# Attention: the values' products of two steps in one place, and the order of the work around them

## The chip, the core and the metric

The kernel runs on one core of a Trainium2 chip, with TensorE (matrix products), VectorE, ScalarE and GpSimd as computing engines and SyncE as the queue that issues most DMAs. Each engine runs its instructions in the order in which they were written and waits on semaphores for the others. The metric is the device time of one execution in microseconds (us); lower is better. A run is the median of several executions; one further execution is recorded by the profiler.

## The reference

Three stages follow one another. Clustered attention: each query and key is assigned to the nearest of 16 centroids of its head, and only pairs with the same centroid see each other. Then a dense layer (weights given in float64), then a layer of eight experts with a gate.

```python
q_assign = np.argmax(np.einsum('bhsd,hcd->bhsc', q_n, c_n), axis=-1)
k_assign = np.argmax(np.einsum('bhsd,hcd->bhsc', k_n, c_n), axis=-1)
mask = q_assign[:, :, :, None] == k_assign[:, :, None, :]
scores = scale * np.matmul(q, k.transpose(0, 1, 3, 2))
scores = np.where(mask, scores, -1000000000.0)
scores = scores - np.max(scores, axis=-1, keepdims=True)
attn = np.exp(scores)
attn = attn / (np.sum(attn, axis=-1, keepdims=True) + 1e-09)
return np.matmul(attn, v).astype(np.float32)
...
h = x @ w_in
sp = np.where(h > 20.0, h, np.log1p(np.exp(np.minimum(h, 20.0))))
g = h * np.tanh(sp)
return (g @ w_out).astype(np.float32)
```

There are 2 batches of 8 heads, 768 positions, 64 numbers per head. The expert layer is not touched by the change.

## The kernel before

Attention works on pairs of heads, eight pairs (`i` from 0 to 7), and each pair is cut into twelve steps: two halves of the queries (`r`, 384 each) times six blocks of 128 keys (`t`). So there are 96 steps, `s = 12*i + 6*r + t`. A step s does:

- `score(s)`: four products (lines 395 and 398, tile `pst`) into one of two large PSUM buffers that are handed out in turn, then one exponential on ScalarE (line 402) into a tile `P` in SBUF, of which there are four.
- `max_unit(n)`: one maximum of 128 queries over all keys, for a step eleven steps later: two products (line 365, tile `pm`) into the other of the two large buffers, and a reduction on VectorE (line 369). It is written first in its step.
- `pv(s-1)`: the values' product of the step before (line 428, tile `acc`). Each head's 64 columns fill half of the array, so this product runs in another arrangement of TensorE than the 128-column products around it. Behind the sixth block ScalarE copies `acc` to `x` (line 434).
- `add_up(s-1)`: two additions of `P` to the running sum on GpSimd (line 416), for the last three groups of six steps on VectorE.

Once per six steps the sums are multiplied by ones (`norm1`, line 441, tile `psum`, also 64 columns), with a logarithm and an exponential on ScalarE (lines 446, 447) to get a reciprocal `rc`; `norm2` refines it and multiplies (`rs` on VectorE, line 456, and ScalarE, line 464; `x` on GpSimd, lines 455 and 465); `norm3` splits the result in two parts (`xh` on ScalarE, line 476, `xl` on VectorE, line 477).

Once per pair the next pair but one is prepared: `load` of q and k, four `split`s (three transposes, tile `pt`, line 233; a copy on ScalarE, line 239; a subtraction on VectorE, line 240), four `sims` (products with the centroids, tile `psim`, line 251; a copy `cl` on ScalarE, line 257; an addition on VectorE, line 258), two `pick`s (a maximum and the one-hot comparison `e`, lines 267 and 268), `onehot_t` (transposes `pe`, line 277; copy `et`, line 282), two `first`s (a product `pp`, line 291, and `nf` on VectorE, line 292), and `spread`s, which are DMAs (line 353): `qa`, `ka` copy parts of q and k, `qm`, `km` copy the masks from `nf` into the tiles QA and KA that the maxima's products read. `max_put` transposes the maxima (`pmt`, line 374).

Between these, attention converts the float64 weights of the dense layer (class `Narrow`): `last` (line 718) and `bias` (line 712) on ScalarE, then `up` and `sign` on VectorE (lines 725 and 734), chunk by chunk. The small PSUM tiles (`pt`, `psim`, `pe`, `pp`, `pmt`, `psum`, and the conversion's `n32p`) share three banks in turn, so each waits until the one three places before it has been read.

What runs in which step is written out in `plan`: `at(s, f, ...)` puts the call f into step s. `advance` goes through the steps and orders the calls of one step. A function that returns a second part (the subtraction of `split`, the addition of `sims`, `nf`, `xl`) has it called at the start of the next step, behind the first maximum.

Of the kernel before, what the change touches and what calls it, by code (L numbers as in the profile page):

```python
# [169 lines left out]
class Attention:  # L170
# [310 lines left out]
    def plan(self, N):  # L481
# [5 lines left out]
        def at(s, f, *a):  # L487
            if s >= 0:
                steps.setdefault(s, []).append((f, a))
# [4 lines left out]
        for s in range(NS):  # L494
            at(s, self.score, s)
        for s in range(NS):
            at(s + 1, self.pv, s)
            at(s + 1, self.add_up, s)
            if s % 6 == 5:
                for j, f in ((3, self.norm1), (4, self.norm2), (6, self.norm3)):  # L500
                    at(s + j, f, *divmod(s // 6, 2))
        for i in range(NP):
            end = 12 * i - self.AHEAD
# [1 line left out]
                if i + r:  # L505
                    at(unit[12 * i + 6 * r + 5] + 1, self.max_put, i, r)
            base = end - 15 if i > 2 else self.B2
            if i == 1:
                at(0, self.onehot_t, i)
                for g in range(2):  # L510
                    at(1, self.first, i, g)
                for h in range(2):
                    for kind in ("km", "qm"):
                        at(2, self.spread, i, (kind, h))
            if i > 1:
                at(base - 8, self.load, i, "qk")
                for j in range(4):
                    at(base + j, self.split, i, "qk"[j // 2], j % 2)
# [26 lines left out]
        return steps  # L545

    BS = 2
    SOON, SLOTS = (14, 19, 22), (0, 2, 7, 8, 10)
    B2 = 0

    BEFORE = 8
# [85 lines left out]
    def advance(self, upto, more={}):  # L637

        for s in range(self.at, upto):
            todo = self.steps.get(s, [])  # L640
            units = [a for f, a in todo if f == self.max_unit]
            first = [a for f, a in todo if f == self.max_put and a == (0, 1)]
            for a in units[:1]:
                self.max_unit(*a)
            for a in first:
                self.max_put(*a)
            for g in self.late:
                g()
            for g in more.get(s, []):
                g()  # L650
            now = (self.score, self.norm1, self.pv, self.add_up, self.onehot_t, self.first)
            todo = [x for f in now for x in todo if x[0] == f] + [x for x in todo if x[0] not in now]
            late = [f(*a) for f, a in todo if f != self.max_unit and not (f == self.max_put and a in first)]
            for a in units[1:]:
                self.max_unit(*a)
            self.late = [g for g in late if callable(g)]
        self.at = upto


# [1075 lines left out]
```

## Time and profile before

| | |
|---|---|
| median of 3 runs | 788.06 us (787.91 to 789.1) |
| profiled execution | 787.98 us, span 786.1 us |
| TensorE products busy | 753.6 us, 96% |
| VectorE busy | 588.8 us, 75% |
| ScalarE busy | 466.6 us, 59% |
| GpSimd busy | 220.7 us, 28% |
| chain that ended last | TensorE 70%, VectorE 16%, issue 5%, ScalarE 4%, DMA 3% |

The span is the time from the first to the last instruction in the trace; the execution's own time is 1.9 us longer. A busy time is a sum over the whole program, with stages of different kinds in it: attention takes about the first third. A matrix product's time in the trace includes its way through the array, so the time between the starts of two products says more than the duration of one. In the time lines each row gives start and duration in us, the engine, the line, the operation, the tile written and the tiles read, and in brackets how long the engine was idle before it and whose end released it.

### The profile page before, as it was taken

How to read it: one execution, taken by the hardware profiler on the slowest of the kernel's cores; microseconds unless marked ns; L12 is line 12 of the kernel's file. 1: busy time of each engine (PE TensorE's matmuls, PEld its weight loads, DVE VectorE, ACT ScalarE, POOL GpSimd, SP SyncE). 2: the span in 40 equal slices, each digit the busy share in tenths (PEclk: the TensorE clock that was granted, in tenths of full speed). 3: DMA queues.
4: the chain of work that ended last, by engine and by line, in shares of the span. 5: the costliest groups of instructions: out<-in, count | busy, mean ns of one | idle time of the engine just before them, and what ended most of it. 6: DMA issues, size and time to landing. Idle time of an engine off the chain costs nothing.

```text
span 786.1 us, 12515 instructions
## 1 busy us (share of the span) xinstructions
PE 753.6 (96%) x4295; PEld 607.5 (77%) x4297; DVE 588.8 (75%) x1195; ACT 466.6 (59%) x901; POOL 220.7 (28%) x247
## 2 busy tenths in 40 slices
PE   8989999999999989899999999999999999999994
PEld 5656566666654568788989899999888999999993
DVE  6756778879779799999997688788677665666661
ACT  4445778778776766555556454445645655656651
POOL 6256668787792200010000030000231101101110
PEclk9999999999999999999999999999999999999998
DMA  9696698989793539796465456232429867986640
GB/s 200 146 218 132 164 273 249 230 237 250 202 281 120 214 128 341 256 317 229 178 233 182 140 188 196 108 141 74 135 82 282 267 213 215 276 262 222 199 125 22
DMA packets 118694, 155.78 MB, mean 198 GB/s; under 512 B 35006, under 2 KB 82206, under 8 KB 114528
## 3 DMA queue, kind: packets, MB, share of 16 engines
q1 hardware_dynamic: 113952, 131.82, 57.6%
q0 software_dynamic: 4624, 23.09, 7.4%
q8 instruction: 36, 0.59, 0.3%
q14 instruction: 34, 0.28, 0.1%
q10 hardware_dynamic: 48, 0.01, 0.0%
HBM read 93.65 MB, written 42.24 MB: 173 GB/s over the span
## 4 chain that ended last, share of the span: by engine, by line
PE 70%; DVE 16%; issue 5%; ACT 4%; DMA 3%; POOL 1%; SPq 1%; ACTq 0%; POOLq 0%; DVEq 0%
PE ph L852 12%; PE o L913 11%; PE he L1509 9%; PE y L1542 9%; PE acc L428 6%; PE pm L365 4%; PE pst L395 3%; PE pst L398 3%; PE psim L251 3%; DVE m L369 2%; DVE n L867 2%; DVE cut L810 1%; DMA n<-in_moe_w_in_dram 1%; ACT r L877 1%; PE o L1161 1%
## 5 line engine op out<-in xcount | busy, mean ns | idle before, releaser
L810 DVE TENSOR_TENSOR cut<-raw,cut 128x512 fp32r<-128x512 f32 x168 | 110.1, 686 | 26.6 <-ACT cut L809 17.6
L369 DVE TENSOR_REDUCE m<-pm 128x1 f32<-128x768 f32 x96 | 91.0, 954 | 49.3 <-PE pm L365 48.9
L416 POOL TENSOR_TENSOR sum<-sum,P 128x384 f32<-128x384 f32 x104 | 104.3, 1034 | 13.1 <-ACT P L402 10.9
L402 ACT ACTIVATE P<-pst 128x768 f32<-128x768 f32 x96 | 77.7, 809 | 43.2 <-PE pst L398 40.4
L809 ACT ACTIVATE cut<-raw 128x512 fp32r<-128x512 f32 x168 | 98.1, 623 | 2.0 <-DMA raw<-in_moe_w_dram 2.0
L1542 PE MATMUL y<-cut,hy 128*128 128x512 f32 x384 | 99.3, 394 | 0.0
L1509 PE MATMUL he<-xeh,cut 128*128 128x256 f32 x512 | 92.5, 280 | 0.2 <-ACT xeh L1463 0.2
L877 ACT ACTIVATE r<-n,two 128x384 f32<-128x384 f32 x64 | 39.5, 617 | 81.1 <-DVE n L867 80.1
L1509 PEld LDWEIGHTS he<-xeh,cut 128*128 128x128 f32 x512 | 82.2, 188 | 5.5 <-ACT xeh L1463 0.4
L428 PE MATMUL acc<-P,vn 128*64 128x384 f32 x384 | 82.4, 508 | 0.1
L1542 PEld LDWEIGHTS y<-cut,hy 128*128 128x128 f32 x384 | 67.6, 188 | 10.9
L852 PE MATMUL ph<-xh,cut 128*128 128x384 f32 x256 | 67.1, 343 | 5.8 <-DVE t L889 3.5
L1509 PE MATMUL he<-xel,cut 128*128 128x256 f32 x256 | 71.5, 279 | 0.2 <-DVE xel L1464 0.2
L395 PE MATMUL pst<-QB,KB 128*128 128x384 f32 x192 | 67.1, 349 | 4.7 <-DVE m L369 3.5
L1514 ACT ACTIVATE hy<-he 128x256 fp32r<-128x256 f32 x64 | 24.5, 383 | 71.7 <-PE he L1509 71.7
L1554 POOL DMA_INDIRECT out_dram<-ye,meta x17 | 18.3, 1077 | 171.6 <-ACT ye L1552 156.9
L852 PE MATMUL ph<-xh,again 128*128 128x384 f32 x256 | 66.1, 339 | 0.0
L398 PE MATMUL pst<-QA,KA 97*128 97x384 f32 x192 | 64.9, 338 | 0.0
L913 PE MATMUL o<-cut,gh 128*128 128x512 f32 x192 | 59.8, 392 | 1.0 <-DVE rs L456 1.0
L1515 DVE SCALAR_TENSOR_TENSOR hy<-he,hy 128x256 fp32r<-128x256 f32 x64 | 27.1, 423 | 44.7 <-ACT hy L1514 44.7
L913 PE MATMUL o<-again,gh 128*128 128x512 f32 x192 | 59.6, 392 | 0.0
L365 PE MATMUL pm<-KA,QA 96*128 96x384 f32 x192 | 54.1, 369 | 2.8 <-DVE m L369 2.7
(238 smaller groups left out, 1616.1 us busy)
## 6 DMA issues: line engine op xcount, KB each, us to landing
raw<-in_moe_w_dram SPq DMA_DIRECT2D x72, 256.0 KB
raw<-in_moe_w_dram SPq DMA_DIRECT2D x36, 512.0 KB
kept<-cut POOLq DMA_DIRECT2D x16, 1024.0 KB, 8.5
again<-kept SPq DMA_DIRECT2D x16, 1024.0 KB
n<-in_moe_w_in_dram SPq DMA_DIRECT2D x16, 512.0 KB
n<-in_moe_w_out_dram SPq DMA_DIRECT2D x16, 512.0 KB
wf<-n SPq DMA_DIRECT2D x32, 256.0 KB
raw<-wf SPq DMA_DIRECT2D x16, 512.0 KB
```

The source lines that it names most:

```text
L365: nc.tensor.matmul(ps[:, g, 0:384], lhsT=QA[0:96, h, q0:q0 + 128], rhs=KA[0:96, h, 384 * g:384 * g + 384], start=True, stop=True,)
L369: nc.vector.reduce_max(out=self.mx[r][:, 3 * h + t:3 * h + t + 1], in_=ps[:, :, 0:384], axis=AX.XY)
L395: nc.tensor.matmul(ps[:, h, 0:384], lhsT=KB[:, h, ks], rhs=QB[:, h, qs], start=True, stop=False)
L398: nc.tensor.matmul(ps[:, h, 0:384], lhsT=KA[0:97, h, ks], rhs=QA[0:97, h, qs], start=False, stop=True)
L416: e.tensor_add(out=o[:, h], in0=a[:, h], in1=b[:, h])
L428: nc.tensor.matmul(acc[64 * h:64 * h + 64, 0:384], lhsT=st["v"][:, h, t, :], rhs=pt[:, h, :], start=(t == 0), stop=(t == self.NK - 1),)
L809: nc.scalar.activation(out=t[:, 0, part], in_=raw[:, part], func=AF.Copy)
L810: self.low.tensor_sub(out=t[:, 1, part], in0=raw[:, part], in1=f32(t[:, 0, part]))
L852: nc.tensor.matmul(ps[:, 0:384], lhsT=w[:, k, :], rhs=x[:, k, sl], start=(k == 0 and j == 0), stop=(k == 3 and j == 2),)
L913: nc.tensor.matmul(self.acc[t], lhsT=g[:, c], rhs=w, start=(f == 0 and j == 0), stop=(f == self.NF - 1 and j == 2),)
L1509: nc.tensor.matmul(ps[:, 0:MAIN], lhsT=w[:, k, :], rhs=x[:, k, :], start=(k == 0 and j == 0), stop=(k == 3 and j == 2),)
L1542: nc.tensor.matmul(st["y"][s], lhsT=g[:, c], rhs=w, start=(f == 0 and j == 0), stop=(f == 7 and j == 2))
```

## The change

The constant `TWO = 24, 72` marks the steps that it rewrites.

- In them the values' product of an even step is put one step later, so that the even steps hold two (of the step two before and of the step before) and the odd steps none.
- `norm2` moves into the step of `norm1`, as the last thing in it; `norm3` comes one step earlier.
- For the pairs from 4 on the preparation is laid out anew: q and k are loaded one step earlier; the four splits stand in steps -3, -1, 1 and 2 (from `base`, instead of 0 to 3), the four centroid products in 3, 4, 5 and 7 (instead of 4 to 7), the one-hot transposes one step later, both `first`s together two and one steps later, and the masks' DMAs (`km`, `qm`) one step later.
- In even steps the second part of `split` and `sims` is called at once instead of in the next step.
- The float64 conversions go from the places 0, 2, 7, 8, 10 of each twelve steps to 1, 3, 5, 7, 10.

```diff
--- before.py
+++ after.py
@@ -494,10 +494,12 @@
         for s in range(NS):
             at(s, self.score, s)
         for s in range(NS):
-            at(s + 1, self.pv, s)
+            two = self.TWO[0] <= s < self.TWO[1]
+            at(s + 2 if two and s % 2 == 0 else s + 1, self.pv, s)
             at(s + 1, self.add_up, s)
             if s % 6 == 5:
-                for j, f in ((3, self.norm1), (4, self.norm2), (6, self.norm3)):
+                two = self.TWO[0] <= s < self.TWO[1] - 6
+                for j, f in ((3, self.norm1), (3 if two else 4, self.norm2), (5 if two else 6, self.norm3)):
                     at(s + j, f, *divmod(s // 6, 2))
         for i in range(NP):
             end = 12 * i - self.AHEAD
@@ -505,14 +507,29 @@
                 if i + r:
                     at(unit[12 * i + 6 * r + 5] + 1, self.max_put, i, r)
             base = end - 15 if i > 2 else self.B2
-            if i == 1:
+            if 12 * i > self.TWO[0] + 12:
+                at(base - 9, self.load, i, "qk")
+                for f, js in ((self.split, (-3, -1, 1, 2)), (self.sims, (3, 4, 5, 7))):
+                    for n, j in enumerate(js):
+                        at(base + j, f, i, "qk"[n // 2], n % 2)
+                at(base + 6, self.pick, i, "q")
+                at(base + 8, self.pick, i, "k")
+                at(base + 10, self.onehot_t, i)
+                for g in range(2):
+                    at(base + 12, self.first, i, g)
+                for h in range(2):
+                    for kind in ("qa", "ka"):
+                        at(base + 8, self.spread, i, (kind, h))
+                    for kind in ("km", "qm"):
+                        at(base + 13, self.spread, i, (kind, h))
+            elif i == 1:
                 at(0, self.onehot_t, i)
                 for g in range(2):
                     at(1, self.first, i, g)
                 for h in range(2):
                     for kind in ("km", "qm"):
                         at(2, self.spread, i, (kind, h))
-            if i > 1:
+            elif i > 1:
                 at(base - 8, self.load, i, "qk")
                 for j in range(4):
                     at(base + j, self.split, i, "qk"[j // 2], j % 2)
@@ -545,7 +562,8 @@
         return steps
 
     BS = 2
-    SOON, SLOTS = (14, 19, 22), (0, 2, 7, 8, 10)
+    SOON, SLOTS = (14, 19, 22), (1, 3, 5, 7, 10)
+    TWO = 24, 72
     B2 = 0
 
     BEFORE = 8
@@ -649,11 +667,24 @@
             for g in more.get(s, []):
                 g()
             now = (self.score, self.norm1, self.pv, self.add_up, self.onehot_t, self.first)
-            todo = [x for f in now for x in todo if x[0] == f] + [x for x in todo if x[0] not in now]
-            late = [f(*a) for f, a in todo if f != self.max_unit and not (f == self.max_put and a in first)]
+            two = s % 2 == 0 and self.TWO[0] <= s < self.TWO[1]
+            end = (self.norm2,) if two else ()
+            todo = (
+                [x for f in now for x in todo if x[0] == f] + [x for x in todo if x[0] not in now + end]
+                + [x for x in todo if x[0] in end]
+            )
+            self.late = []
+            for f, a in todo:
+                if f == self.max_unit or f == self.max_put and a in first:
+                    continue
+                g = f(*a)
+                if callable(g):
+                    if two and f in (self.split, self.sims):
+                        g()
+                    else:
+                        self.late.append(g)
             for a in units[1:]:
                 self.max_unit(*a)
-            self.late = [g for g in late if callable(g)]
         self.at = upto
```

How this moves instructions shows in three places; the changed file is longer, so lines 712 to 734 of the kernel before are 743 to 765 in it. On TensorE in steps 42 and 43, before (`acc` is a values' product, two for one step; `pm` maxima, `pst` scores, `pe` one-hot transposes):

```order
L428 MATMUL acc<-P,vn_1207 64x384 x2
L365 MATMUL pm<-KA_99,QA_98 128x384 x2
L395 MATMUL pst<-QB_102,KB_103 128x384
L398 MATMUL pst<-QA_96,KA_97 128x384
L395 MATMUL pst<-QB_102,KB_103 128x384
L398 MATMUL pst<-QA_96,KA_97 128x384
L428 MATMUL acc<-P,vn_1207 64x384 x2
L277 LDWEIGHTS e_1739
```

and after (`pmt` the maxima's transpose, `pt` a split's transposes):

```order
L428 MATMUL acc<-P,vn_1213 64x384 x4
L365 MATMUL pm<-KA_99,QA_98 128x384 x2
L395 MATMUL pst<-QB_102,KB_103 128x384
L398 MATMUL pst<-QA_96,KA_97 128x384
L395 MATMUL pst<-QB_102,KB_103 128x384
L398 MATMUL pst<-QA_96,KA_97 128x384
L374 MATMUL pmt<-ident,m_106 128x128
L233 MATMUL pt<-ident,qn_1633 128x128 x3
L365 MATMUL pm<-KA_99,QA_98 128x384 x2
L395 MATMUL pst<-QB_102,KB_103 128x384
```

Four products to `acc` now stand together in step 42, and step 43 has none between its scores and the next maxima.

On ScalarE around the sums of steps 43 to 45, before (`et` is the one-hot copy, `n_...` and `n32p` the conversion, `rc` the sums' logarithm and exponential, `rs` the normalisation's second part, `P` a step's exponential):

```order
L402 ACTIVATE P<-pst 128x768
L282 ACTIVATE et_105<-pe 64x768
L376 ACTIVATE mt<-pmt 6x128
L712 ACTIVATE n32p<-n_11_1602 128x512
L402 ACTIVATE P<-pst 128x768
L446 ACTIVATE rc<-psum,eps 128x384
L447 ACTIVATE rc<-rc 128x384
L718 ACTIVATE n_12_1678<-n_12_1678 128x512
L402 ACTIVATE P<-pst 128x768
L464 ACTIVATE rs<-rs,neg 128x384
```

and after:

```order
L402 ACTIVATE P<-pst 128x768
L446 ACTIVATE rc<-psum,eps 128x384
L447 ACTIVATE rc<-rc 128x384
L282 ACTIVATE et_105<-pe 64x768
L749 ACTIVATE n_12_1717<-n_12_1717 128x512
L464 ACTIVATE rs<-rs,neg 128x384
L402 ACTIVATE P<-pst 128x768
```

The one-hot copy, a conversion and the normalisation's second part now stand in one row between two exponentials.

On VectorE around the masks `nf` of pair 5, before (`m` is the reduction of the maxima, `ql` a split's subtraction, `xl` the normalisation's split):

```order
L292 TENSOR_SCALAR nf<-pp,fb 64x384
L456 SCALAR_TENSOR_TENSOR rs<-psum,rc 128x384
L369 TENSOR_REDUCE m_107<-pm 128x1
L292 TENSOR_SCALAR nf<-pp,fb 64x384
L725 SCALAR_TENSOR_TENSOR n32p<-n32p,n_12_1678 128x512
L734 SCALAR_TENSOR_TENSOR n_12_1922<-n_12_1678,n32p 128x512
L369 TENSOR_REDUCE m_107<-pm 128x1
```

and after:

```order
L240 TENSOR_TENSOR ql_1827<-pt,qh_1826 128x384
L756 SCALAR_TENSOR_TENSOR n32p<-n32p,n_12_1717 128x512
L765 SCALAR_TENSOR_TENSOR n_12_1924<-n_12_1717,n32p 128x512
L369 TENSOR_REDUCE m_107<-pm 128x1
L292 TENSOR_SCALAR nf<-pp,fb 64x384 x2
L477 SCALAR_TENSOR_TENSOR xl_75<-x,xh_73 128x384
L369 TENSOR_REDUCE m_107<-pm 128x1
```

Both halves of `nf` now stand behind the reduction that follows the conversion, and the reductions between the halves are gone.

## Rows read from the trace of the kernel before

**Rows 1.** Busy time by stretch: length, each engine (instructions), granted clock, DMA share, GB/s
```profile
97.38:222.15 124.77, 123.60 (x692) 78.97 (x692) 102.21 (x159) 96.78 (x172) 94.69 (x96) 1.00 0.90 241
222.20:250.80 28.60, 26.69 (x132) 15.10 (x131) 24.35 (x34) 19.73 (x33) 17.86 (x18) 1.00 0.60 180
```

**Rows 2.** Time line of TensorE: first score product of steps 36 and 48
```profile
128.09 0.34 PE L395 MATMUL pst<-QB,KB 128*128 128x384 f32 x1
...
159.57 0.34 PE L395 MATMUL pst<-QB,KB 128*128 128x384 f32 x1
```

**Rows 3.** Time line of TensorE (start, duration, line, tile): steps 57 to 59, 64
```profile
182.07 0.87 PE L441 MATMUL psum<-sum,ones 128*64 128x384 f32 x4
182.76 0.81 PE L428 MATMUL acc<-P,vn 128*64 128x384 f32 x4
...
187.14 0.87 PE L428 MATMUL acc<-P,vn 128*64 128x384 f32 x4
187.94 0.55 PE L233 MATMUL pt<-ident,qn 128*128 128x128 f32 x3
188.24 0.60 PE L365 MATMUL pm<-KA,QA 96*128 96x384 f32 x2
188.68 0.34 PE L395 MATMUL pst<-QB,KB 128*128 128x384 f32 x1
...
189.47 0.87 PE L428 MATMUL acc<-P,vn 128*64 128x384 f32 x4
...
201.49 0.39 PE L251 MATMUL psim<-cc,qh 128*128 128x256 f32 x1
...
202.31 0.51 PE L365 MATMUL pm<-KA,QA 96*128 96x384 f32 x2
202.66 0.34 PE L395 MATMUL pst<-QB,KB 128*128 128x384 f32 x1
```

**Rows 4.** Time lines of TensorE, ScalarE, VectorE: who waits for whose end
```profile
164.59 0.62 PE L365 MATMUL pm<-KA,QA 96*128 96x384 f32 x2 [0.32 <-DVE m L369]
...
246.53 0.79 ACT L402 ACTIVATE P<-pst 128x768 f32<-128x768 f32 x1
...
247.38 0.45 PE L395 MATMUL pst<-QB,KB 128*128 128x384 f32 x1 [0.41 <-ACT P L402]
...
248.39 0.81 ACT L402 ACTIVATE P<-pst 128x768 f32<-128x768 f32 x1 [1.06 <-PE pst L398]
...
249.28 0.96 DVE L369 TENSOR_REDUCE m<-pm 128x1 f32<-128x768 f32 x1
...
250.29 0.62 PE L365 MATMUL pm<-KA,QA 96*128 96x384 f32 x2 [1.14 <-DVE m L369]
```

**Rows 5.** Groups of instructions, 97.4 to 222.2 (total, mean ns | idle before)
```profile
L725 DVE SCALAR_TENSOR_TENSOR n32p<-n32p,n 128x512 int32<-128x512 int32 x20 | 13.8, 690 | 0.0
...
L718 ACT ACTIVATE n<-n 128x512 int32<-128x512 uint8 x20 | 13.3, 667 | 0.0
...
L464 ACT ACTIVATE rs<-rs,neg 128x384 f32<-128x384 f32 x8 | 4.9, 617 | 1.7 <-DVE rs L456 1.6
...
L282 ACT ACTIVATE et<-pe 64x768 bf16<-64x768 bf16 x4 | 3.2, 804 | 0.3
```

**Rows 6.** Time line of VectorE: one-hot comparison in steps 52 and 54
```profile
172.96 1.23 DVE L268 TENSOR_TENSOR e<-qs,mx 128x192 bf16<-128x192 f32 x1
...
178.98 0.36 DVE L268 TENSOR_TENSOR e<-ks,mx 128x192 bf16<-128x192 f32 x1
```

**Rows 7.** Time lines of the DMA queue, VectorE, TensorE: issues and first uses
```profile
0.81 0.39 SPq L128 DMA_DIRECT2D cn<-in_centroids_dram  x1
...
2.58 0.22 DVE L135 TENSOR_TENSOR cn<-cn 128x64 f32<-128x64 f32 x1 [0.72 <-DMA cn<-in_centroids_dram]
...
220.11 0.59 SPq L353 DMA_DIRECT2D QA<-nf  x1
...
223.74 0.62 PE L365 MATMUL pm<-KA,QA 96*128 96x384 f32 x2
```

## The prediction

> **What bounds the kernel now.** I read the busy time by stretch first, then TensorE's line of time step by step, then the vector and scalar engines beside it. I call the start of a step's first score product the step's start. Steps 24 to 72, which the change rewrites, run from 97.38 to 222.15: 124.8 us, 31.2 per twelve steps; TensorE is busy for 123.6 of it, VectorE for 102.2, ScalarE for 96.8 and GpSimd for 94.7, at a granted clock of 1.00, its upper level of 2.4 GHz [rows 1]. So attention is bound by TensorE, but three engines that work in strict order stand beside it at more than three quarters. The twelve steps from step 36 take 31.48 [rows 2].
>
> A bare step is three pieces [rows 3]: from the maxima's first product to the scores' first 0.44 us (0.35 where no values' product came just before), the four score products and the crossing to the values' product 0.79, and the values' product up to the next 128-column product 0.80. That is 2.03. The last two numbers hold the price of entering and leaving the 64-column arrangement. A second product inside one such episode costs less: from the sums' product to the values' product behind it is 0.69. A split's transposes cost 0.30, a centroid product 0.82 behind an episode and some 0.7 elsewhere [rows 3].
>
> **The saving on TensorE.** Two bare steps cost 4.06. With both values' products in the even step, the odd one shrinks to 0.35 + 0.70 = 1.05 (two products take 0.35, and the crossing falls away), and the even one grows to 2.03 + 0.69 = 2.72: 3.77, so 0.29 saved per pair, and 24 pairs would give 7.0 us if TensorE bounded each step. In the odd ones it doesn't.
>
> **The floor of an odd step.** Maxima and scores take turns in two PSUM buffers, so a step's scores can't start before the exponential of the step before has read its buffer. The exponential starts 1.01 after the start of scores that had to wait (their first product then lasts 0.45 instead of 0.34, so 0.90 otherwise), lasts 0.8, and the next scores start 0.06 after its end [rows 3, 4]. That makes 1.77 from scores to scores, however little TensorE has to do. Odd steps that hold a centroid product (1.05 + 0.7) fill this just so; those with a split (1.35) leave TensorE waiting 0.4, and a product that waits costs another 0.1 by the same row. The maxima have a floor of the same kind, 0.6 for the products, 0.96 for the reduction and 0.05 to the next maxima [rows 3, 4].
>
> **Twelve steps laid out.** I lay these durations on the new order, with step 36 at 0, and follow for each pair of steps what ends last.
> - 36 and 37: the even step is 3.0 (2.72 and a split). VectorE now subtracts the second split in the same step and waits for its transposes and copy until 3.4; so the reduction of step 37 starts at 3.9 instead of 3.2, and the maxima of step 38 at 4.9 instead of 4.5. Pair 5.3.
> - 38 and 39: sums' product, two values' products, centroid product, 4.2. Behind the sums ScalarE holds in a row the logarithm, the exponential, a copy that waits for the centroid product, a float64 conversion, and the normalisation's second part (0.62 [rows 5]), which waits for VectorE, which waits for that same centroid product. Only then comes step 39's exponential, 0.5 late. Pair 6.5.
> - 40 and 41: 4.6. 42 and 43: 4.6. The float64 work behind the odd maxima pushes the even reduction late, and the long even step absorbs it.
> - 44 and 45: sums, two values' products and the one-hot transposes end 3.5 after the start; then on ScalarE the one-hot copy 0.80, a conversion 0.67, the normalisation's 0.62 [rows 5], and behind them step 45's exponential, 0.6 late. Pair 6.2.
> - 46 and 47: 4.9.
> Sum 32.1, against 31.48: **plus 0.6 per twelve steps**. Against the 1.7 that six pairs save stand 1.2 from the odd floor under the three split steps, 0.5 and 0.6 from the two late exponentials, 0.4 from the late reduction and five waits of 0.1; a wait that the present order has once in twelve steps (0.32 and its 0.1 [rows 4]) is in the 31.48.
>
> **Beside GpSimd.** The one-hot comparison took 1.23 us beside GpSimd's sums and 0.36 apart from them [rows 6]. In the new order it falls into step 40, and the split of the normalised values, which I take to be of the same two kinds, into step 41, just where GpSimd, after waiting for the normalisation, catches up with its sums. Both long would push the reduction of step 42 by 0.9, of which 0.75 reaches TensorE; both short, nothing. I take 0.4, the middle. The Trainium skill's page SBUF — State Buffer (the practical consequences of its shared port pair) says that a VectorE instruction with two SBUF inputs and a GpSimd instruction that reads SBUF exclude each other for a whole instruction; by it all would be long and the time 1.4 us above my sum, while the pair of rows shows both kinds.
>
> So steps 24 to 72 change by 4 x (0.6 + 0.4) = **plus 4.0**, between plus 2.4 and plus 5.4. The first twelve still have the old normalisation, but no present wait to lose; the last twelve have no splits, but the same floor. I count them alike.
>
> **The masks' copies.** The step nf (both halves) moves behind the reduction of the step two ahead of a pair's first maxima, and the DMAs that spread it one step later, behind a float64 load. Now the copy's issue ends at 220.70, and the maxima that need it start at 223.74 without waiting for it [rows 7], so landing takes at most 3.0. The least is the centroids' load, the one small transfer whose landing a wait shows: its issue ended at 1.20, the waiting VectorE started at 2.58, 1.4 [rows 7]. In the new order the issue ends 1.7 after the start of step 48 and the maxima of step 49 want the copy at 2.6. A landing in 1.4 costs nearly nothing, since the reduction of that step is late anyway; each 0.1 more costs 0.1, at steps 37, 49, 61 and 73. Between 0.1 and 6.5 in all; I take a landing of 1.8, nearer the measured transfer: **plus 1.7**.
>
> **Behind step 72** sums run on VectorE: it is busy for 24.35 of 28.60 us, TensorE for 26.69 [rows 1], and a reduction holds the maxima for 1.14 [rows 4]. The new slots take one pair of float64 operations (2 x 0.69 [rows 5]) from step 80 to 77. Between nothing and 1.4 comes back; I take half, **minus 0.7**.
>
> **Edits at nothing.** Loads of q and k go one step earlier and stand six steps ahead of their first use instead of eight, still some 15 us. The even splits' earlier subtraction frees banks for the next sums. Products delayed by one step hold one more P buffer, three of four. Each cover is gone only if steps shrink to a third.
>
> **The sum.** The profiled run took 787.98 (the span's 786.1 and 1.9 around it), 0.08 under the median. 787.98 + 4.0 + 1.7 - 0.7 = 793.0.
>
> **Rivals.**
> (a) Faster: the odd steps keep near their floor. If the exponentials of steps 39 and 45 come on time (ScalarE's copies done some tenths sooner than my durations allow), the 1.1 goes and with it 0.5 of waits that follow: 30.5 instead of 32.1. That is 0.7 less than the present 31.2 per twelve steps, minus 2.8; with the landing hidden and minus 0.7 behind step 72, 784.5. It decides at 0.3 per odd step above the floor: below that the change gains. With every odd step at 1.77 and 19.4 for the six even ones, 30.0: minus 4.8, 782.5.
> (b) No change: half of that lateness, 786.5 to 789.5.
> (c) Much slower: the copies land at their upper end, 793.0 + 4.8 = 797.8, with all comparisons long 799.2. For it: the DMA engines are 0.90 busy there [rows 1].
> (d) The change doesn't do what it says: the second values' product pays for an episode of its own. Then 0.29 x 24 more, 800. Against it stands the 0.69.
> The Trainium skill (DMA: Bandwidth & Descriptors, on the anatomy of one DMA) gives about 2 us of fixed cost for a DMA of GpSimd's queue; as an estimate for this queue it would put the copies' term at plus 2.5 and the time at 793.8. No run here shows it for this queue.
>
> **Chances.** My forecast, slower by 2 to 8 us, 0.47; (c) 0.11; (d) 0.01; (b) 0.17; (a) 0.24. A measurement of this kernel tells some 0.2%, 1.6 us, from no change. Faster 0.24, same 0.17, slower 0.59. The range goes from 784 to 798.5.
>
> **What would show it.** Right: in the profile after, steps 24 to 72 last about 129 us; score products wait for the exponential behind odd steps, which none does there now; the exponentials of steps 39, 45, 51 and 57 start 1.4 or more after their scores; odd steps with splits last 1.8 to 1.9. Wrong: odd steps of 1.8 throughout and a stretch under 123 us mean (a); maxima that wait over 0.5 us at steps 37, 49 and 61 for copies of nf mean (c); values' products 0.8 apart inside an even step mean (d).

## The result and the profile after

| | before | after |
|---|---|---|
| median of 4 runs | 787.98 us (787.67 to 789.1) | 798.25 us (797.34 to 801.96) |
| ratio to the kernel before | | 1.0136, 95% interval 1.011 to 1.0162 |
| profiled execution, span | 787.98 us, 786.1 | 798.96 us, 797.1 |

The change makes the kernel slower by 10.3 us. The forecast was plus 5.0 with a range up to 798.5: the sign and the range held, but what came is twice what was summed. A few executions, two of the twelve with four pairs and one in each longer row of the kernel before, ran in a slower state; ratios and intervals leave them out.

The busy time by stretch (length, then the busy time and instructions of TensorE, its weight loads, VectorE, ScalarE and GpSimd, granted clock, DMA share, GB/s), for steps 24 to 72 and 72 to 84:

```profile
98.12:231.55 133.43, 124.09 (x684) 82.27 (x683) 101.66 (x158) 92.65 (x170) 95.00 (x95) 0.99 0.86 228
231.55:261.35 29.80, 27.27 (x136) 15.52 (x135) 24.30 (x35) 20.57 (x34) 18.12 (x18) 1.00 0.56 159
```

Against [rows 1] the first stretch is 8.7 us longer, yet TensorE is busy for only half a microsecond more (part of that from a few microseconds at the lower clock, below): the time went into TensorE's waits. What it waited for from 97 us to step 73 (engine and line that waited, for whose end: us in total, times, longest):

```profile
PE pm L365 <- DVE m L369: 4.1, 7, 1.2
PE pm L365 <- DMA QA<-nf: 1.9, 3, 0.9
PE pst L395 <- ACT P L402: 1.7, 4, 0.4
PE psim L251 <- DVE rs L456: 1.0, 1, 1.0
PE pm L365 <- DMA KA<-nf: 0.8, 1, 0.8
```

The same view of the kernel before has one line, the first, with 1.2 us. Three of the four others are waits that the prediction looked for, the fourth (1.0 for `rs`) is step 27, which keeps the old normalisation.

TensorE's first score products of steps 36 and 48 (start and duration in us) are 33.15 apart, where [rows 2] have 31.48:

```profile
130.21 0.44 PE L395 MATMUL pst<-QB,KB 128*128 128x384 f32 x1
...
163.36 0.44 PE L395 MATMUL pst<-QB,KB 128*128 128x384 f32 x1
```

The floor of an odd step, step 45, on TensorE's time line and on ScalarE's; a bracket is the idle time ahead and what ended it:

```profile
156.20 0.34 PE L395 MATMUL pst<-QB,KB 128*128 128x384 f32 x1
...
157.41 0.62 PE L365 MATMUL pm<-KA,QA 96*128 96x384 f32 x2
158.46 0.44 PE L395 MATMUL pst<-QB,KB 128*128 128x384 f32 x1 [0.43 <-ACT P L402]
```

```profile
157.12 0.60 ACT L464 ACTIVATE rs<-rs,neg 128x384 f32<-128x384 f32 x1
157.62 0.79 ACT L402 ACTIVATE P<-pst 128x768 f32<-128x768 f32 x1
```

The scores begin at 156.20, the exponential that empties their buffer only at 157.62, behind the one-hot copy, the conversion and the normalisation; the next scores begin at 158.46. This is the late exponential that the prediction laid out.

What it sized too small: the reduction of step 43, on VectorE's time line and, last line, TensorE's.

```profile
146.10 0.93 DVE L477 SCALAR_TENSOR_TENSOR xl<-x,xh 128x384 fp32r<-128x384 f32 x1
...
149.82 1.20 DVE L268 TENSOR_TENSOR e<-ks,mx 128x192 bf16<-128x192 f32 x1
150.94 0.94 DVE L369 TENSOR_REDUCE m<-pm 128x1 f32<-128x768 f32 x1
```

```profile
151.94 0.62 PE L365 MATMUL pm<-KA,QA 96*128 96x384 f32 x2 [0.88 <-DVE m L369]
```

`xl` took 0.93 and, behind the float64 work and another reduction, the comparison of the keys 1.20; the maxima's products waited 0.88 behind them. In [rows 6] the keys' comparison took 0.36. The comparison that the prediction had in mind here, that of the queries in step 40, takes 0.43 in this trace.

The masks' copies, on SyncE's queue and on TensorE, at steps 36 and 72:

```profile
131.32 0.58 SPq L353 DMA_DIRECT2D QA<-nf  x1
...
232.66 0.58 SPq L353 DMA_DIRECT2D QA<-nf  x1
```

```profile
133.53 0.59 PE L365 MATMUL pm<-KA,QA 96*128 96x384 f32 x2 [0.43 <-DMA QA<-nf]
...
234.91 0.59 PE L365 MATMUL pm<-KA,QA 96*128 96x384 f32 x2 [0.95 <-DMA QA<-nf]
```

From the end of the issue (131.90, 233.24) to the product that waited are 1.63 and 1.67 us; at steps 48 and 60 it was 2.00 and 1.69. (At step 48 the view names the copy to KA, issued just ahead of that to QA; the 2.00 is counted from QA's, the later of the two.) In [rows 7] nothing waited for such a copy.

Last, something that the prediction doesn't have. TensorE's time line at step 68, and the stretch behind it in the view by stretch:

```profile
218.69 0.62 PE L365 MATMUL pm<-KA,QA 96*128 96x384 f32 x2 [1.23 <-DVE m L369]
...
219.70 0.52 PE L395 MATMUL pst<-QB,KB 128*128 128x384 f32 x1
220.47 1.55 PE L441 MATMUL psum<-sum,ones 128*64 128x384 f32 x4
```

```profile
219.40:223.60 4.20, 4.20 (x18) 1.95 (x17) 1.78 (x3) 1.91 (x3) 1.20 (x2) 0.61 1.02 226
```

After a wait of 1.23 the granted clock fell to its lower level: a score product takes 0.52 instead of 0.34, the sums' product 1.55 instead of 0.87 [rows 3], and step 68 lasts 5.26 where steps 44 and 56 last 3.80 and 3.78. That is 1.5 us in this execution. Of the four executions two took 797.3 and 797.6 and two 799.0 (the profiled one) and 802.0; the prediction's sum is compared below with the profiled one.

### The profile page after: what moved, and what is told of

It reads as the page before. It is cut to its first block, busy times and chain, and to the rows that moved or that the text cites. A ratio compares the mean times of both kernels' runs of the same rounds, so it can differ in the third digit from the quotient of the medians.

```text
span 797.1 us, 12520 instructions
## 1 busy us (share of the span) xinstructions
PE 755.2 (95%) x4297; PEld 611.3 (77%) x4297; DVE 588.5 (74%) x1195; ACT 463.2 (58%) x901; POOL 221.8 (28%) x247
## 4 chain that ended last, share of the span: by engine, by line
PE 63%; DVE 15%; DMA 7%; issue 6%; ACT 6%; SPq 1%; POOL 0%; ACTq 0%; POOLq 0%; DVEq 0%
PE ph L883 12%; PE o L944 11%; PE he L1540 9%; PE y L1573 9%; PE acc L428 5%; PE pm L365 3%; DVE m L369 3%; PE pst L395 2%; PE pst L398 2%; PE psim L251 2%; DMA n<-in_moe_w_in_dram 1%; DVE n L898 1%; DVE cut L841 1%; ACT r L908 1%; DMA QB<-qh 1%
## 5 line engine op out<-in xcount | busy, mean ns | idle before, releaser
L428 PE MATMUL acc<-P,vn 128*64 128x384 f32 x384 | 77.6, 504 | 0.1
L395 PE MATMUL pst<-QB,KB 128*128 128x384 f32 x192 | 69.0, 360 | 6.3 <-DVE m L369 3.5
```

The source lines that it names most:

```text
L395: nc.tensor.matmul(ps[:, h, 0:384], lhsT=KB[:, h, ks], rhs=QB[:, h, qs], start=True, stop=False)
L428: nc.tensor.matmul(acc[64 * h:64 * h + 64, 0:384], lhsT=st["v"][:, h, t, :], rhs=pt[:, h, :], start=(t == 0), stop=(t == self.NK - 1),)
```

## The experiments

**The pairing alone.** The kernel before, and in steps 24 to 72 only the products put together:

```diff
-            at(s + 1, self.pv, s)
+            two = self.TWO[0] <= s < self.TWO[1]
+            at(s + 2 if two and s % 2 == 0 else s + 1, self.pv, s)
```

> The kernel before with one thing of the change: the values' products of two steps together in even steps 24 to 72; all other work where it was. If the score buffer sets a floor of 1.78 us under every odd step (my theory), the products alone can't gain: TensorE's content of odd steps is 1.05 to 1.75, so twelve steps cost about 31.2 to 31.9 instead of 31.2, and the time is 788 to 791. If TensorE alone counted, 24 pairs would give 7 us, 781. If pairing itself carried the loss of the whole change, 796 or more.

Measured: 788.76 us, ratio 1.0007 (0.9998 to 1.0017). TensorE's time line at step 37, which no longer holds a values' product:

```profile
131.56 0.34 PE L395 MATMUL pst<-QB,KB 128*128 128x384 f32 x1
...
133.40 0.45 PE L395 MATMUL pst<-QB,KB 128*128 128x384 f32 x1
```

From scores to scores are 1.84, and the second one shows the 0.45 of a product that had to wait. From step 27 on the odd steps last 1.77 to 2.00 (step 25 keeps its 2.48); the six pairs of one twelve give 31.3 instead of 31.48. So the theory of the floor gave the time: the 7 us that TensorE saves by its own durations don't come, and the floor takes nearly all of them. But the pairing by itself doesn't cost the 10 us either.

**The moves alone.** The changed kernel with each values' product one step behind its scores again:

```diff
-            at(s + 2 if two and s % 2 == 0 else s + 1, self.pv, s)
+            at(s + 1, self.pv, s)
```

> The changed kernel with each step's values' product in the next step again, as before; all moves of the other work are kept. My theory: steps are then over 2.0 us long, late exponentials fit under them, and what is left of the loss is the wait for the masks' copies (up to 0.85 us at steps 37, 49, 61 and 73) and 0.7 in steps 19 to 23, less the waits of 0.4 that the order of before had: 789 to 791. The rival, that the moves carry the loss whatever the products do: 796 to 798.

Measured: 802.25 us, ratio 1.017 (1.0149 to 1.019). My expectation fell; by the medians the moves are 4 us worse without the pairing than with it, though the two intervals still touch. SyncE's queue (first two lines) and TensorE's time line at steps 36 and 37, then two stretches of the view by stretch:

```profile
129.64 0.38 SPq L726 DMA_DIRECT2D n<-in_moe_w_in_dram  x1
...
131.14 0.58 SPq L353 DMA_DIRECT2D QA<-nf  x1
```

```profile
131.61 0.44 PE L398 MATMUL pst<-QA,KA 97*128 97x384 f32 x1 [2.12 <-DMA QA<-mt]
...
136.85 0.63 PE L365 MATMUL pm<-KA,QA 96*128 96x384 f32 x2 [3.17 <-DMA QA<-nf]
```

```profile
129.20:137.30 8.10, 2.81 (x15) 1.46 (x14) 3.00 (x4) 3.07 (x6) 3.89 (x4) 1.00 0.93 257
137.30:141.60 4.30, 4.30 (x18) 2.68 (x17) 2.25 (x3) 1.23 (x4) 1.83 (x2) 0.61 0.43 106
```

Here the same copy needs 5.1 us (131.72 to 136.85): a load of 512 KB of float64 weights was issued 1.5 us ahead of it, another 2 us before that, and the DMA engines are 0.93 busy. Behind the wait the clock is at its lower level. Step 36 lasts 8.13 us and step 37 4.33. So the upper end that I gave a landing (3.0) is not one. The wait of 2.12 at 131.61 is for another copy, `mt`, that feeds the scores.

**The moves alone with the float64 conversions in their old places:**

```diff
-    SOON, SLOTS = (14, 19, 22), (1, 3, 5, 7, 10)
+    SOON, SLOTS = (14, 19, 22), (0, 2, 7, 8, 10)
```

> The moves without the pairing (802 us), with the float64 conversions back in their old places. Theory that the new places put the weights' loads, 512 KB each, ahead of the masks' copies, which then land some 5 us after their issue: 791 to 794 and no wait over 1 us for copies of nf. Theory that the later copies alone do it: 798 or more, with the same waits.

Measured: 796.47 us, ratio 1.0106 (1.0091 to 1.0121), between the two. Its waits for the copies on TensorE, in the view of waits:

```profile
PE pm L365 <- DMA QA<-nf: 2.9, 3, 1.5
```

The wait at step 48, 0.7, is put to `kl` and not to a copy, but `kl` had ended just ahead of a copy's landing. With it the waits at steps 36, 48, 60 and 72 are 0.64, 0.71, 0.73 and 1.50, 3.6 us; counted alike, those of the moves alone are 5.3 (2.1 of it for `mt`), 3.4, 1.1 and 1.4, 11.2 us. With the loads elsewhere the landing waits so fall by 7.7 us and the time by 5.8. That part of the moves' cost is shown to hang on the float64 places.

Of the remaining 8 us against the kernel before, the copies are 3.6 and steps 19 to 23 another 0.75. Step 39 and its fellows last 3.59 instead of 2.77, but the step behind them, which lost a centroid product, 2.15 instead of 2.77. What makes step 39 long stands on VectorE's time line, the float64 work and the normalisation ahead of the reduction that the next maxima wait for (0.35, until 143.25):

```profile
141.18 0.69 DVE L765 SCALAR_TENSOR_TENSOR n<-n,n32p 128x512 int32<-128x512 int32 x1
141.78 0.55 DVE L456 SCALAR_TENSOR_TENSOR rs<-psum,rc 128x384 f32<-128x384 f32 x1
142.25 0.95 DVE L369 TENSOR_REDUCE m<-pm 128x1 f32<-128x768 f32 x1
```

The rest, some 3 us, is spread over many steps by tenths.

**The float64 places in the changed kernel.** The same edit, with the pairing:

> The changed kernel with the float64 conversions back in the places 0, 2, 7, 8, 10 of each twelve steps. Theory that the new places put the loads of the weights right ahead of the masks' copies and so carry the copies' term (3 us): 795 to 796.5, and no wait for copies of nf. Theory that the conversions' VectorE work has to stand behind the odd maxima, because the even step now holds both values' products, a split's subtraction and the normalisation: the even reductions come later, 800 or more.

Measured: 803.55 us, ratio 1.0197 (1.0181 to 1.0214). The second theory holds in its direction, by another wait than the one it named. The view of waits:

```profile
PE psim L251 <- DVE n L765: 6.1, 7, 1.3
```

Centroid products wait 6.1 us for the float64 sign on VectorE, because the conversion takes one of the three small banks and the product needs it back; steps 37 and 39 last 2.93 and 3.59 instead of 1.88 and 2.25. Step 43, where the new places cost something, falls from 2.66 to 2.01. With the pairing the move of the conversions is worth 5.3 us, without it, it costs 5.8.

**The preparation in its old steps.** The changed kernel without the new layout of pairs 4 to 7:

```diff
-            if 12 * i > self.TWO[0] + 12:
+            if False:
```

> The changed kernel with the preparation of the pairs 4 to 7 in its old steps (loads, splits, centroid products, one-hot transposes, nf, masks' DMAs), all else as changed. Theory that the later masks' copies and the splits in steps 19, 21 and 23 carry 3.7 us of the loss: 794.5 (793 to 796.5), no wait for copies of nf, steps 19 to 23 as in the kernel before. Theory that the loss sits in the float64 places and the preparation was laid out to fit them: 798 or more, with products that wait for the float64 sign.

Measured: 806.97 us, ratio 1.0256 (1.0223 to 1.0289). The time is on the second theory's side, the mechanism is neither's. The view of waits, then VectorE's time line at step 41:

```profile
PE pm L365 <- DVE m L369: 11.6, 11, 2.0
```

```profile
148.97 0.26 DVE L258 TENSOR_TENSOR ks<-cl,psim 128x96 f32<-128x96 f32 x1 [1.88 <-ACT cl L257]
...
149.52 1.22 DVE L268 TENSOR_TENSOR e<-qs,mx 128x192 bf16<-128x192 f32 x1
150.66 0.94 DVE L369 TENSOR_REDUCE m<-pm 128x1 f32<-128x768 f32 x1
```

VectorE stands 1.88 idle for the copy of a centroid product, with the comparison and the reduction queued behind it, and step 41 lasts 3.33 instead of 1.78; the granted clock over steps 24 to 72 is 0.96. So the new layout costs some 3.5 us of its own (copies, steps 19 to 23), but the paired order with the old one costs 8.7 more, part of it by the lower clock.

**The normalisation in its old steps:**

```diff
-                for j, f in ((3, self.norm1), (3 if two else 4, self.norm2), (5 if two else 6, self.norm3)):
+                for j, f in ((3, self.norm1), (4, self.norm2), (6, self.norm3)):
```

> The changed kernel with the normalisation's second part and split back in their old steps. Theory that the second part in the sums' own step delays the exponentials of steps 39 and 45 by 0.5 but spares a longer wait (in the changed kernel's step 27, which still has the old order, a centroid product waits 1.0 for it and the step lasts 3.00 against 2.25 in step 39): 800 us (799 to 803). Theory that the lateness is what the move costs: 794 (793 to 796).

Measured: 798.84 us, ratio 1.0127 (1.0112 to 1.0142): no difference from the changed kernel. TensorE's time line:

```profile
141.50 0.36 PE L251 MATMUL psim<-cc,kh 128*128 128x256 f32 x1 [0.99 <-DVE rs L456]
...
167.51 0.69 PE L365 MATMUL pm<-KA,QA 96*128 96x384 f32 x2 [2.17 <-DMA KA<-nf]
```

Step 39 grows from 2.25 to 2.99 as the first theory has it, and steps 45, 57 and 69 fall from 2.26 to 1.83, since their exponential comes on time; step 43 falls to 2.00, because `xl` no longer stands ahead of its reduction. The sum of one twelve (36 to 48) is 32.57 instead of 33.15, and a copy that landed late at step 48 (a wait of 2.17, where the changed kernel has 0.81) took it back in the profiled execution. The late exponential is thus real and in itself avoidable, but only for a wait elsewhere.

**The keys' comparison one step later**, behind the reduction that it delays:

```diff
-                at(base + 8, self.pick, i, "k")
+                at(base + 9, self.pick, i, "k")
```

> The changed kernel with the one-hot comparison of the keys (and the maximum ahead of it) one step later, so that it stands behind the odd step's reduction of the maxima instead of ahead of it. If that comparison, 1.20 us beside GpSimd's sums, is what makes step 43 and its like 2.66 us long, those steps go to 1.8 and the time falls by 2.5 to 3.5, to about 795. If the steps are long for another reason (the float64 work, the wait for the even reduction), nothing changes: 798.

Measured: 798.74 us, ratio 1.0143 (1.012 to 1.0167). Step 43 falls from 2.66 to 1.84, so the comparison is what delays it (written behind the reduction, it takes 0.36), but TensorE's time line at step 44 has a new wait:

```profile
153.45 0.87 PE L441 MATMUL psum<-sum,ones 128*64 128x384 f32 x4 [0.47 <-DVE n L765]
```

The comparison now stands ahead of the float64 sign, and the sums' product needs that bank: step 44 lasts 4.28 instead of 3.80. The cause is shown, and so is that the 0.8 can't be had there for more than 0.3.

**The masks one step earlier:**

```diff
-                    at(base + 12, self.first, i, g)
+                    at(base + 11, self.first, i, g)
...
-                        at(base + 13, self.spread, i, (kind, h))
+                        at(base + 12, self.spread, i, (kind, h))
```

> The changed kernel with the two mask products of pairs 4 to 7 one step earlier (in the odd step, under its floor) and the masks' DMAs one step earlier. If the maxima of steps 37, 49, 61 and 73 wait for the landing of those copies, the waits of 0.4 to 0.95 go, step 72 goes from 3.8 to under 2.8, and the even step that held the mask products shrinks by 0.3: minus 3 to minus 4.2, about 794.5. If the copies were covered by the late reduction there, only the 0.3 is seen, 797.

Measured: 796.84 us, ratio 1.0114 (1.0097 to 1.0131). Steps 36, 48, 60 and 72 fall from 3.75, 4.12, 3.80 and 3.78 to 2.99, 2.98, 2.99 and 2.79: the landing wait is gone. But steps 47 and 37 grow from 1.78 and 1.88 to 2.22 and 2.31. VectorE's time line and, last, TensorE's:

```profile
126.07 1.13 DVE L292 TENSOR_SCALAR nf<-pp,fb 64x384 fp32r<-64x384 f32 x2
...
128.91 0.95 DVE L369 TENSOR_REDUCE m<-pm 128x1 f32<-128x768 f32 x1
```

```profile
129.91 0.62 PE L365 MATMUL pm<-KA,QA 96*128 96x384 f32 x2 [0.47 <-DMA QA<-nf]
```

The bracket names a copy of nf, but that can't be it: this is the last maximum of the pair before, which doesn't read the new masks, and the reduction ended at 129.86, 0.05 before. `nf`, the subtraction and the float64 work now stand in a row ahead of that reduction. So the copies cost what their waits show, as the first theory has it, but moving them back gives only 1.4 us by the medians, by intervals that overlap, since the new waits take the rest.

**The exponential in two halves**, in the odd steps of the changed kernel and, as a control, of the kernel before:

```diff
-        nc.scalar.activation(out=pt, in_=ps[:, :, 0:384], func=AF.Exp, scale=1.0 / float(self.D) ** 0.5)
+        halves = (0, 1) if s % 2 and self.TWO[0] <= s < self.TWO[1] else (slice(0, 2),)
+        for h in halves:
+            nc.scalar.activation(out=pt[:, h], in_=ps[:, h, 0:384], func=AF.Exp, scale=1.0 / float(self.D) ** 0.5)
```

> The changed kernel with the exponential of each odd step of 24 to 72 written as two halves, one head each, so that the whole ends 0.1 to 0.2 us later. Theory of the floor: five of six odd steps (all but the seventh of each twelve, whose end the late reduction sets) are bound from exponential to exponential, so each is longer by just that: 20 times 0.15, plus 3.0 us (2 to 4). Theory that TensorE bounds the odd steps or that only the reductions hold it: under 0.6.

> The same two halves in the odd steps 24 to 72 of the kernel before, the control. Theory of the floor: its odd steps last 2.2 to 3.1 us, above 1.77, so the longer exponential is hidden: plus 0 to 0.5 us. If the halves cost something by themselves (ScalarE's own time), as much as in the changed kernel.

Measured: 800.64 us (797.73 to 804.01), ratio 1.0168 (1.0136 to 1.0199), and for the control 788.1, ratio 0.9997 (0.9987 to 1.0006). The time of the first doesn't tell: its interval overlaps the changed kernel's. The steps do. ScalarE's and TensorE's time lines at step 41:

```profile
146.09 0.87 ACT L404 ACTIVATE P<-pst 128x384 f32<-128x384 f32 x2 [0.91 <-PE pst L398]
```

```profile
145.17 0.34 PE L395 MATMUL pst<-QB,KB 128*128 128x384 f32 x1
...
147.01 0.45 PE L395 MATMUL pst<-QB,KB 128*128 128x384 f32 x1
```

The two halves last 0.87 instead of 0.81, less than I expected, and the step 1.84 instead of 1.78. Fifteen odd steps grow by 0.04 to 0.07; those that something else ends (the first and seventh of each twelve, and step 27) don't; in the control none does. So the floor from exponential to exponential is shown step by step, with 0.9 in all where the theory had 3.0. The profiled total is not even that, because even steps that wait for a copy or a reduction anyway give it back.

**Pairing where it pays.** The kernel before with three pairs of six:

```diff
-            at(s + 1, self.pv, s)
+            two = self.TWO[0] <= s < self.TWO[1] and s % 12 in self.PAIRS
+            at(s + 2 if two else s + 1, self.pv, s)
...
+    TWO, PAIRS = (24, 72), (0, 2, 4)
```

> The kernel before with the pairing alone, and that only in three of each six pairs: where the odd step holds a split or a centroid product that fills it (steps 0 and 1, 2 and 3, 4 and 5 of each twelve). Theory of the floor (a pair gains only if its odd step had 0.3 us or more above 1.77 besides its values' product): with the pairing in every pair these three changed by -0.58, -0.17 and -0.26, the other three by +0.29, +0.35 and +0.18; so four times -1.0, 784 us (783.5 to 785). Theory that the gains and losses of neighbouring pairs depend on each other (a step that is late takes its time from the next): 787 to 788.5, no change.

Measured: 788.98 us, ratio 1.0011 (1.0001 to 1.0021): no gain, the second theory. Step 37 kept its 3.14 us. VectorE's and TensorE's time lines there:

```profile
129.91 1.24 DVE L477 SCALAR_TENSOR_TENSOR xl<-x,xh 128x384 fp32r<-128x384 f32 x1
```

```profile
133.00 0.55 PE L233 MATMUL pt<-ident,kn 128*128 128x128 f32 x3 [0.83 <-DVE n L736]
```

VectorE is late there (1.24 for `xl`, then a subtraction and the float64 work), and the split's transposes wait for the bank. With all six pairs step 36 is longer by 0.7 and `xl` comes apart from GpSimd's sums (0.60), so that wait is gone. Hence a fourth pair, the one that makes step 36 longer:

```diff
-    TWO, PAIRS = (24, 72), (0, 2, 4)
+    TWO, PAIRS = (22, 70), (10, 0, 2, 4)
```

> The kernel before with the pairing alone, now in four of six pairs, from step 22 on: the three of the run before, whose odd steps are 1, 3 and 5 of each twelve as far as the saving goes (3 and 5 gave -0.19 and -0.25 there), and the one ahead of them, whose shorter odd step 11 brings step 0 forward. With three pairs step 1 kept its 3.13 us, because its split's product waits 0.83 for the float64 sign, which stands on VectorE behind a split of the normalised values that took 1.24 us there; with all pairs paired that wait was gone. Theory that step 1 loses its wait as soon as the pair ahead of it is formed: 0.18 lost there, 0.55, 0.18 and 0.25 gained, four times -0.8, 785 us (784.5 to 786.5). Theory that the shift helps only where all six are paired, or is given back in the next pair: 787.5 to 789, no change.

Measured: 786.73 us, ratio 0.9975 (0.9966 to 0.9984), faster than both kernels. Steps 24 to 72, in the view by stretch:

```profile
97.85:221.23 123.38, 121.53 (x696) 80.90 (x695) 100.15 (x159) 93.83 (x173) 96.46 (x96) 1.00 0.92 244
```

1.4 us less than in [rows 1]; step 37 lasts 1.85, and no product waits for the float64 sign. Half of the 3.2 that I had added up from the pairs comes, and the half that fails lies at the ends. The twelves from steps 36 and 48 are shorter by 0.65 and 0.60, near the 0.8 of the theory; the one from step 60, without its last pair, by 0.31, and the one from step 24 is longer by 0.18: its step 25 had 2.48 and no such wait to lose. The time lies just above the first theory's range.

## Why the prediction was right in sign and half in size

By the profiled executions the change is plus 11.0 us of span, where the sum has plus 5.0. The mechanism held, the floor, the late exponentials and the late copies; what failed is the size of its terms. The largest miss is the term for steps 24 to 72: plus 4.0 was summed from four twelves counted alike, and plus 6.1 came. The masks' copies took 2.7 instead of 1.7, and the splits that the new layout puts ahead of step 24 stood at nothing and took 0.75. The forecast itself was slower by 2 to 8; that 798.25 lies inside the range at all is luck, since the range reaches so far only for rival (c).

**The floor of an odd step: right.** 1.77 was predicted; steps 41, 47, 53, 59, 65 last 1.78 or 1.79, and the halved exponential lengthens them by just its own 0.06. The pairing alone gains nothing: although the exponentials of steps 39 and 45 start 0.97 and 0.96 after their scores there, it is 788.8, not the 784.5 of rival (a). The stretch was to last about 129 us; it lasts 133.4, or 132.0 without the clock's fall.

**The six pairs from step 36: five right.** Predicted 5.3, 6.5, 4.6, 4.6, 6.2, 4.9; measured 5.63 (0.43 of it the landing), 6.39, 4.58, 5.59, 6.06, 4.90. The fourth holds what was summed beside GpSimd, below; without that 1.0 and the landing the six come to 31.7, less than the 32.1 laid out, and so hide a part of the next miss. The exponentials of steps 39, 45, 51 and 57 start 1.41 to 1.43 after their scores, as the text asked.

**Beside GpSimd: mis-sized.** I took 0.4 as the middle between both instructions long and both short, and the pair at steps 42 and 43 shows 1.0. The text had the queries' comparison and `xl` hold up the reduction of step 42. It was another pair and another reduction: `xl` (0.93) and the keys' comparison (1.20) held up that of step 43, as the run with the later comparison shows, while the queries' comparison, which took 1.23 in [rows 6], takes 0.43. That GpSimd's sums make the difference is read from the time lines; no run took the sums away. The rule of the Trainium skill's page SBUF — State Buffer, in the practical consequences of its shared port pair, had both long, and here the trace agrees for `xl` and the keys; the 0.43 stands beside GpSimd's sums too, so the rule is no price for each instruction.

**Twelve steps counted alike: wrong at the ends.** Without the landings and the lower clock, steps 36 to 48 and 48 to 60 are longer by 1.24 and 1.29, near the 1.0 of the sum. The first twelve are longer by 1.38, with step 27's wait of 1.0 for the old normalisation. The last twelve are longer by 1.58: in the kernel before step 70 has no split and lasts 2.05 against 2.33 in step 46, in the changed one both last 3.12. And step 72 gets the second product of the last pair, 0.62 more in the pairing alone between steps 72 and 84. Together 6.1 instead of 4.0.

**The masks' copies: right in mechanism, 1.0 short.** The issue ends 1.7 after the start of step 48 as laid out, and the landing of 1.63 to 2.00 is near the 1.8 taken. But the four waits are 0.43, 0.81, 0.48 and 0.95, 2.7 instead of 1.7: at step 48 the landing was the longest, and at step 73 no split stands ahead of the maxima to cover it. Rival (c) gave 797.8, close to the time, for a reason that the trace doesn't show here: landings of 3.0 and more come only in other kernels of this study. Of the waits that were to mean (c), over 0.5 us, there is one among the three named (0.81).

**Behind step 72: half.** Steps 81 and 82 gain 0.58 and step 76 loses 0.24: minus 0.35 instead of minus 0.7.

**Not in the sum at all.** Steps 19 to 23 are longer by 0.75: the new layout moves pair 4's splits into 19 and 21, 0.3 each, ahead of the paired steps, step 22 loses one, and the late reduction of step 23 puts the maxima behind it 0.45 later. My list of edits at nothing had the loads of that layout, not the splits ahead of step 24 (0.2 of it comes back in step 25). The clock's fall costs 1.45 in this execution. A last 0.4 lies behind step 84, and I have no cause for it.

So 6.1 + 2.7 - 0.35 + 0.75 + 1.45 + 0.4 is some 11.0. Two executions took 797.3 and 797.6 at a mean granted clock of 0.995, where the profiled one had 0.993; taken as free of the clock's fall, they lose some 9.5, and the terms miss 4.5: steps 24 to 72 2.1, copies 1.0, splits 0.75, steps 76 to 82 0.35, the rest unexplained.

**Rival (d)** falls: the two values' products of step 36 start 0.69 apart (131.11 and 131.80), as the 0.69 of [rows 3].

**What stays open.** What decides whether the clock falls behind a wait; some 3 of the 8 us that the moves cost without the pairing and with the old float64 places; and whether 793 would be reached if comparison, copies and ends were all mended at once, since each mend tried alone made a new wait.

## What to carry to other kernels

A saving on the busiest engine counts only in steps that end on it: write down for each step the loop through the buffers (here exponential to exponential, 1.77 us) and put the saving only where the step is longer, as the four pairs did. An order in which several engines stand at three quarters is fitted as a whole: the float64 move cost 5.8 us without the pairing and was worth 5.3 with it, so neither sign can be read from a part alone. And lay out the first and the last period too, with everything that a moved block issues ahead of the range.

## What the hardware showed that was not expected

- The granted clock fell to its lower level behind waits of TensorE of 1.23 us (step 68 after) and 3.17 us (moves alone), 0.61 over the next four microseconds. In the run with three pairs, whose profiled execution took 791.36 against a median of 788.98, it fell behind a wait of 1.15; in the kernel before a wait of 1.14 [rows 4] is not followed by it, nor are one of 1.21 ahead of step 68 with the masks early and one of 1.50 ahead of step 73 (moves alone, float64 in its old places): the granted clock stays at 1.00 behind them.
- The landing of the same small copy on SyncE's queue took 1.63 to 2.00 us in the changed kernel. It took 5.1 and 4.25 (moves alone, steps 36 and 48) and 3.4 us (normalisation in its old steps, step 48) where two 512 KB loads had been issued within the 4.5 us ahead of its issue, the later one 1.5, 2.4 and 3.1 ahead. With one such load 2.5 to 2.7 ahead it took 1.66 and 1.74 (moves alone with the float64 work in its old places, steps 36 and 48) and 2.00 (moves alone, step 60). So the distance to the last load alone does not set it; what does is open. The Trainium skill's page DMA: Bandwidth & Descriptors, on the anatomy of one DMA, has about 2 us of fixed cost for a DMA of GpSimd's queue; for SyncE's queue the runs show values near it in most places, and these three beyond it.
- The same comparison takes 0.36 or 1.2 us depending on its place beside GpSimd's sums: in the kernel before 1.23 amid sums that follow one another, 0.36 where none runs. In the changed kernel the queries' comparison of step 40 takes 0.43 at the seam of two sums, and the later of them lasts 1.14 instead of 1.00. The mean of the four in steps 24 to 72 (total, mean ns) changes sides between the kernels; before, then after:

```profile
L268 DVE TENSOR_TENSOR e<-qs,mx 128x192 bf16<-128x192 f32 x4 | 4.0, 1008 | 0.1
L268 DVE TENSOR_TENSOR e<-ks,mx 128x192 bf16<-128x192 f32 x4 | 1.4, 358 | 0.1
```

```profile
L268 DVE TENSOR_TENSOR e<-ks,mx 128x192 bf16<-128x192 f32 x4 | 4.0, 994 | 0.1
L268 DVE TENSOR_TENSOR e<-qs,mx 128x192 bf16<-128x192 f32 x4 | 2.4, 588 | 0.1
```
